# Low parts of the first products' weights: subtraction on DVE instead of POOL

## The chip, the cores and the metric

The kernel runs on one core of one Trainium2 chip. The time is device microseconds (us) from launch to end. PE is the matrix engine (TensorE), DVE the vector engine, ACT the scalar engine, POOL is GpSimd, and SP the engine that issues the DMAs. "L329" is line 329 of the kernel.

## What is computed

Attention with a memory term, then a small gated network on its output, all in fp32 (B = 4, H = 8, S = 576, D = 64):

```python
scores = q @ k.T / sqrt(D)                  # causal
a = exp(scores - rowmax); a /= a.sum(-1) + 1e-9
local = a @ v
q_p = elu(q) + 1
mem = (q_p @ M_prev) / ((q_p * z_prev).sum(-1) + 1e-6)
x = g * mem + (1 - g) * local               # g = sigmoid(beta), per head
h = (x @ w1) * (x @ w2)                     # 512 -> 1024
out = (h @ w3) @ w_out                      # 1024 -> 1024 -> 512
```

The weights are handed over as float64 words. Their 64 bits are read as pairs of 32-bit words, and the kernel itself makes fp32 numbers of them.

## The kernel before

**Pairs.** Attention runs over 16 pairs of heads (`pair_step`, four pairs for each of four batches). A pair's step writes instructions by a table, `ORDER`: transposes of the normalised scores (`t_mm`, L236, copied to SBUF by ACT in L267), the products with `v` (`pv_mm`, L283), the evacuation `fin`, and for the next pair the scores (`s_all`: L205 and L191 on PE, row maxima by L182 on DVE), the exponentials (`s_exp`, L217 on ACT), the normalisation (`s_norm`: L221, L222, L226 on DVE) and the memory term (`mem_a` to `mem_c`, `mem_t`: L138 and L139 on ACT, L144, L151 to L157 on DVE, L146 and L159 on POOL, transposes L165 on PE). `fin` evacuates a PSUM tile `x` twice: ACT writes a rounded high part (L294), DVE the rest (L295). There is one such PSUM tile, and the score tile `sx` of the next pair takes its place.

**Weights.** `w3 @ w_out` is made once (`w_gen`, L429 on PE, with high parts by L434 on ACT and low parts by L421 on DVE), beside the first batch's attention. The products with w1 and w2 (`gemm1`, L479) start with the second batch. Each operand of `gemm1` is a high part and a low part, and three products are added. Their results leave PSUM by L485 (ACT) and L488 (DVE).

**Conversion.** `conv_stages` turns a block of 128x512 float64 numbers into fp32, as a job in four stages: `load` (a DMA, L305, into `wst`), `scale` (ACT, L316, into a staging tile `wp`), `join` (DVE, L320 and L321) and `split`. Jobs 0 to 23 are w_out and w3 and have no split. Jobs 24 to 39 are w1 and w2, two for each of eight tiles `wsp`; their split writes the high part by ACT (L328) and the low part by POOL (L329). `conv_tick` moves three jobs on by one stage each, and six letters `c` in `ORDER` call it. The `wp` tiles rotate: two tiles of tag "o" (jobs 24, 25, 28, 29, 32, 33, 36 and on) and two others (26, 30, 34 and 27, 31, 35). So L316 of a job waits until L329 of the job before it in the same tile has read it. The `wst` tiles rotate by three: the load of job k waits for L321 of job k-3.

In the lists below the numbered names stand for jobs: `wp_847` is 27, `wp_989` 29, `wp_1011` 30, `wp_1026` 31, `wp_1177` 32, `wp_1185` 33, `wp_1223` 34, `wp_1231` 35, `wp_1267` 36.

**Order.** The code is written as one stream; a scheduler places each instruction in its engine's queue by priorities, and each engine then works its queue in order. `tc.high_priority` lifts L294, L295, L434, L485 and L488.

Of the kernel before, what the change touches and what calls it, by code (L numbers as in the profile page):

```python
# [13 lines left out]
ALU = mybir.AluOpType  # L14
# [23 lines left out]
def f32(ap):  # L38
    return ap.bitcast(F32)
# [3 lines left out]
def attention_moe_kernel(  # L43
# [13 lines left out]
    nc = tc.nc  # L57
# [240 lines left out]
    def conv_stages(k, src, dh, dl):  # L298
        n = 512
        box = {}  # L300

        def load():
            t = x_p.tile([128, 2 * S], F32, tag=f"x{4 + k % 3}", name="wst")
            box["raw"] = t[:, 0:2 * n].bitcast(U32).rearrange("p (n w) -> p n w", w=2)
            nc.sync.dma_start(out=t[:, 0:2 * n].bitcast(U32), in_=src.bitcast(U32))  # L305

        def scale():
            if k < 24:
                box["raw"] = raws[src[0]][:, src[1]]
            if k < 24:  # L310
                box["p"] = dh()
            elif k < 36 and k % 4 > 1:
                box["p"] = big.tile([128, n], F32, tag=f"r{4 + k % 4}", name="wp")
            else:
                box["p"] = o_p.tile([128, n], F32, tag="o", name="wp")
            nc.scalar.activation(out=box["p"], in_=f32(box["raw"][:, :, 1]), func=ACTF.Prelu, scale=2.0 ** -111, alpha=-(2.0 ** 32))  # L316

        def join():
            p = box["p"].bitcast(U32)
            nc.vector.tensor_scalar(out=p, in0=p, scalar1=3, scalar2=None, op0=ALU.logical_shift_left)  # L320
            nc.vector.scalar_tensor_tensor(  # L321
                out=p, in0=box["raw"][:, :, 0], scalar=29, in1=p, op0=ALU.logical_shift_right, op1=ALU.bitwise_or
            )

        def split():
            if k < 24:
                return
            nc.scalar.activation(out=dh(), in_=box["p"], func=ACTF.Copy)  # L328
            nc.gpsimd.tensor_tensor(out=dl(), in0=box["p"], in1=f32(dh()), op=ALU.subtract)  # L329

        return load, scale, join, split

# [216 lines left out]
    def pair_step(p, F):  # L549
# [46 lines left out]
        out=mask[:, 448:576], in_=mask[:, 448:576], pattern=[[-1, 128]], compare_op=ALU.is_ge,  # L596
# [96 lines left out]
```

## Time and profile before

| | us |
|---|---|
| median of 3 runs (lowest, highest) | 572.43 (571.6, 573.46) |
| the profiled execution | 571.37 |
| its span, first to last instruction | 569.6 |
| PE busy | 545.4 (96%) |
| DVE / ACT busy | 279.4 / 277.5 (49% each) |
| POOL busy | 126.6 (22%) |

The views below give times in us from the start of the span. A busy PE need not be a PE at its full clock; the granted clock is a column of its own, as a share of the full one.

### The profile page before, as it was taken

What the parts mean: (1) busy time and instruction counts of PE and PEld (TensorE: products, weight loads), DVE (VectorE), ACT (ScalarE), POOL (GpSimd) and SP (SyncE); (2) the same over time, 40 slices, a digit from 0 to 9 for tenths busy, and PEclk for the clock granted to TensorE, in tenths of its full rate; (3) what the DMA queues carried; (4) which work ended last, traced back from release to release, by engine and by line L of the source; (5) the groups of instructions that cost most, each with busy time, mean ns of one, the idle gap of its engine ahead of it and who ended that gap; (6) DMA issues with size and microseconds to landing.
All of it is one profiled execution on the core that took longest, in us unless ns stands there. A gap on an engine that the chain in (4) does not pass through costs nothing.

```text
span 569.6 us, 9266 instructions
## 1 busy us (share of the span) xinstructions
PE 545.4 (96%) x3440; PEld 436.4 (77%) x3440; DVE 279.4 (49%) x880; ACT 277.5 (49%) x723; POOL 126.6 (22%) x153
## 2 busy tenths in 40 slices
PE   4899897899999999999999999999999999999997
PEld 2344554456797889788988898797969797998995
DVE  6986797838662626263726272724535351111111
ACT  5565785648562546454644455444635362130210
POOL 1101333015613032303230313021310320130220
PEclk9899989799999999999999999999999999999999
DMA  7991653713021312130202121322012000001001
GB/s 292 421 379 49 223 181 121 223 48 102 31 68 29 105 29 67 34 109 29 66 20 92 29 68 34 91 64 68 26 36 99 23 1 6 33 1 38 1 1 55
DMA packets 23069, 48.31 MB, mean 85 GB/s; under 512 B 6896, under 2 KB 13040, under 8 KB 21488
## 3 DMA queue, kind: packets, MB, share of 16 engines
q1 hardware_dynamic: 23024, 47.72, 25.1%
q8 instruction: 27, 0.44, 0.3%
q14 instruction: 18, 0.15, 0.1%
HBM read 43.00 MB, written 4.72 MB: 84 GB/s over the span
## 4 chain that ended last, share of the span: by engine, by line
PE 82%; DVE 8%; ACT 4%; issue 2%; POOL 2%; DMA 2%; SPq 0%; POOLq 0%; DVEq 0%
PE m L479 36%; PE m L499 18%; PE x L283 7%; PE s L236 7%; PE s L205 4%; PE m L429 4%; PE x L274 2%; PE sx L205 2%; DVE sm L226 2%; PE x L165 1%; DVE sm L182 1%; POOL wsp L329 1%; DMA wst<-w_out 1%; ACT pt L267 1%; PE s L191 1%
## 5 line engine op out<-in xcount | busy, mean ns | idle before, releaser
L479 PE MATMUL m<-xs,wsp 128*128 128x288 f32 x1536 | 221.6, 299 | 1.3 <-DVE wL L421 1.3
L479 PEld LDWEIGHTS m<-xs,wsp 128*128 128x128 f32 x1536 | 206.7, 188 | 2.3 <-DVE wL L421 1.5
L491 POOL TENSOR_TENSOR ht<-a,ht 128x288 fp32r<-128x288 f32 (+2 forms) x96 | 57.6, 612 | 237.5 <-ACT ht L490 237.5
L217 ACT ACTIVATE sm<-sm,mx 128x320 f32<-128x320 f32 (+2 forms) x144 | 82.7, 576 | 39.5 <-DVE mx L182 38.5
L499 PE MATMUL m<-wH,ht 128*128 128x512 f32 x288 | 94.2, 396 | 0.0
L488 DVE SCALAR_TENSOR_TENSOR a<-m,a 128x288 f32<-128x288 f32 x64 | 29.1, 455 | 99.1 <-PE m L479 94.7
L267 ACT ACTIVATE pt<-s 128x512 f32<-128x512 f32 (+1 forms) x144 | 63.3, 492 | 25.1 <-PE s L236 25.0
L429 PE MATMUL m<-wo,w3s 128*128 128x512 f32 x128 | 65.5, 647 | 6.2 <-DVE w3s L321 3.8
L499 PEld LDWEIGHTS m<-wH,ht 128*128 128x128 f32 x288 | 54.1, 188 | 11.2
L490 ACT ACTIVATE ht<-a 128x288 fp32r<-128x288 f32 (+2 forms) x96 | 31.5, 360 | 63.2 <-DVE a L488 63.1
L236 PE MATMUL s<-ident,sm 128*128 128x128 f32 x448 | 61.7, 273 | 0.0
L236 PEld LDWEIGHTS s<-ident,sm 128*128 128x128 f32 x448 | 52.7, 140 | 7.2 <-issue 5.8
L226 DVE TENSOR_SCALAR sm<-sm,sums 128x320 f32<-128x320 f32 (+2 forms) x144 | 57.1, 457 | 0.4
L182 DVE CUSTOM_DVE_ANT_0 sm<-s,mask 128x320 f32<-128x320 f32 (+3 forms) x112 | 44.4, 448 | 24.4 <-PE s L205 24.3
L499 PE MATMUL m<-wL,ht 128*128 128x512 f32 x144 | 56.2, 390 | 0.0
L146 POOL TENSOR_TENSOR e<-qn,z 128x640 f32<-128x640 f32 x16 | 25.3, 1581 | 136.3 <-DVE qn L144 112.9
L485 ACT ACTIVATE a<-m 128x288 f32<-128x288 f32 x64 | 26.1, 408 | 50.7 <-PE m L479 45.4
L429 PEld LDWEIGHTS m<-wo,w3s 128*128 128x128 f32 x128 | 24.4, 209 | 31.3 <-issue 20.0
L283 PEld LDWEIGHTS x<-pt,v 128*64 128x64 f32 x384 | 25.1, 137 | 29.9 <-issue 24.0
L283 PE MATMUL x<-pt,v 128*64 128x448 f32 (+4 forms) x384 | 46.7, 393 | 0.0
L295 DVE TENSOR_TENSOR xs<-x,xs 128x576 fp32r<-128x576 f32 x16 | 12.1, 756 | 66.6 <-ACT xs L294 66.6
L205 PE MATMUL s<-raw 64*128 64x320 f32 (+3 forms) x256 | 38.3, 414 | 4.5 <-DMA raw<-qkt 4.5
(65 smaller groups left out, 474.3 us busy)
## 6 DMA issues: line engine op xcount, KB each, us to landing
raw<-qkt SPq DMA_DIRECT2D x16, 576.0 KB, 3.9
wst<-w3t SPq DMA_DIRECT2D x8, 1024.0 KB, 8.9
wst<-w SPq DMA_DIRECT2D x16, 512.0 KB, 3.8
qn<-qn SPq DMA_DIRECT2D x16, 320.0 KB, 3.0
v<-v SPq DMA_DIRECT2D x32, 160.0 KB, 2.3
out<-o SPq DMA_DIRECT2D x18, 256.0 KB, 2.0
wst<-w_out SPq DMA_DIRECT2D x4, 1024.0 KB, 12.0
z<-z_prev SPq DMA_DIRECT2D x16, 64.0 KB, 2.9
```

The source lines that it names most:

```text
L182: nc.vector.tensor_tensor_reduce(out=sm[a][c][:, lo:hi] if c else sm0[:, 0:64], in0=x, in1=mask[:, S - KE[c] + lo:S - KE[c] + hi] if c els ...
L205: nc.tensor.matmul(y, lhsT=t[r, 0, 128 * c - 64:128 * c + 64], rhs=t[r, 1, lo:hi], start=True, stop=True)
L217: nc.scalar.activation(out=x, in_=x, func=ACTF.Exp, bias=mx, scale=-1.0, accum_out=sums_of(p)[:, k:k + 1])
L226: nc.vector.tensor_scalar(out=x, in0=x, scalar1=sums_of(p)[:, k:k + 1], scalar2=None, op0=ALU.mult)
L236: tr = lambda o, c, a, kc: nc.tensor.transpose(ps[:, o:o + 128], sm[a][c][:, 128 * kc:128 * kc + 128], ident)
L267: nc.scalar.activation(out=d, in_=s, func=ACTF.Copy)
L283: nc.tensor.matmul(x[64 * a:64 * a + 64, 384 + q0:384 + q1], lhsT=vv[:, a, kc], rhs=pt[:, a, o:o + q1 - q0], start=False, stop=(q0 == 0 or ...
L429: nc.tensor.matmul(ps, lhsT=w[:, 128 * kc:128 * kc + 128], rhs=wo[:, 512 * (kc % 2):512 * (kc % 2) + 512], start=(kc == 0), stop=(kc == 7))
L479: nc.tensor.matmul(ps[:, 0:U], lhsT=w[:, i, x, j], rhs=x_t[NC * b + j][:, xx, U * u:U * u + U], start=(k == 0), stop=(k == 11))
L490: nc.scalar.activation(out=hbuf(f, 0)[:, p:p + c], in_=a[:, o:o + c], func=ACTF.Copy)
L491: nc.gpsimd.tensor_tensor(out=hbuf(f, 1)[:, p:p + c], in0=a[:, o:o + c], in1=f32(hbuf(f, 0)[:, p:p + c]), op=ALU.subtract)
L499: nc.tensor.matmul(ps, lhsT=hbuf(f, a)[:, p:p + 128], rhs=b[f], start=(k == 0), stop=(k == 23))
```

## The change

In `split` the subtraction that writes the low part (box minus high part) is issued to DVE and no longer to POOL. The operands, the tiles and the shape (128x512) are the same.

```diff
             if k < 24:
                 return
             nc.scalar.activation(out=dh(), in_=box["p"], func=ACTF.Copy)
-            nc.gpsimd.tensor_tensor(out=dl(), in0=box["p"], in1=f32(dh()), op=ALU.subtract)
+            nc.vector.tensor_tensor(out=dl(), in0=box["p"], in1=f32(dh()), op=ALU.subtract)
```

All sixteen L329 leave POOL's queue for DVE's. PE's queue keeps its order from first to last. The scheduler also moves other instructions of DVE and ACT, in three places above all.

DVE in the third pair's step, from the memory term's L152 on, up to the row maxima of the next pair's scores; `n_907` is the memory term's divisor, `xs_850` the evacuated tile. Before:

```order
L152 TENSOR_SCALAR n_907<-n_907 128x10
L153 RECIPROCAL n_907<-n_907 128x10
L157 TENSOR_TENSOR n_907<-n_907,g_sb_104 128x10
L320 TENSOR_SCALAR wp_1026<-wp_1026 128x512
L321 SCALAR_TENSOR_TENSOR wp_1026<-wst_1009,wp_1026 128x512
L320 TENSOR_SCALAR wp_1011<-wp_1011 128x512
L321 SCALAR_TENSOR_TENSOR wp_1011<-wst_987,wp_1011 128x512
L295 TENSOR_TENSOR xs_850<-x_823,xs_850 128x576
L320 TENSOR_SCALAR wp_1231<-wp_1231 128x512
L321 SCALAR_TENSOR_TENSOR wp_1231<-wst_1221,wp_1231 128x512
L320 TENSOR_SCALAR wp_1223<-wp_1223 128x512
L182 ISA sm02_109,mx_869<-s_854,mask_101 128x320
```

and with the change, with one more L329 (job 29) just ahead of the first row, and one more (job 31) between the last row and L182:

```order
L152 TENSOR_SCALAR n_907<-n_907 128x10
L329 TENSOR_TENSOR wsp_957<-wp_847,wsp_957 128x512
L153 RECIPROCAL n_907<-n_907 128x10
L320 TENSOR_SCALAR wp_1177<-wp_1177 128x512
L157 TENSOR_TENSOR n_907<-n_907,g_sb_104 128x10
L321 SCALAR_TENSOR_TENSOR wp_1177<-wst_1024,wp_1177 128x512
L320 TENSOR_SCALAR wp_1026<-wp_1026 128x512
L321 SCALAR_TENSOR_TENSOR wp_1026<-wst_1009,wp_1026 128x512
L320 TENSOR_SCALAR wp_1011<-wp_1011 128x512
L321 SCALAR_TENSOR_TENSOR wp_1011<-wst_987,wp_1011 128x512
L295 TENSOR_TENSOR xs_850<-x_823,xs_850 128x576
L329 TENSOR_TENSOR wsp_1170<-wp_1011,wsp_1170 128x512
```

The join of job 32 has moved to a place ahead of L295, and the joins of jobs 35 and 34 to places behind the first row maxima.

ACT around the evacuation L294 of the same step. Before:

```order
L328 ACTIVATE wsp_957<-wp_847 128x512
L316 ACTIVATE wp_1026<-wst_1009 128x512
L328 ACTIVATE wsp_1170<-wp_1026 128x512
L316 ACTIVATE wp_1011<-wst_987 128x512
L294 ACTIVATE xs_850<-x_823 128x576
L316 ACTIVATE wp_1231<-wst_1221 128x512
L328 ACTIVATE wsp_1170<-wp_1011 128x512
L316 ACTIVATE wp_1223<-wst_1183 128x512
```

and with the change:

```order
L316 ACTIVATE wp_1177<-wst_1024 128x512
L328 ACTIVATE wsp_957<-wp_847 128x512
L316 ACTIVATE wp_1026<-wst_1009 128x512
L316 ACTIVATE wp_1011<-wst_987 128x512
L294 ACTIVATE xs_850<-x_823 128x576
L328 ACTIVATE wsp_1170<-wp_1026 128x512
L328 ACTIVATE wsp_1170<-wp_1011 128x512
L316 ACTIVATE wp_1231<-wst_1221 128x512
```

L328 of job 31 now stands behind L294.

DVE at the end of the fourth pair's step, where L421 writes the last low part of `w3 @ w_out` (`wL7`). Before:

```order
L226 TENSOR_SCALAR sm14_115<-sm14_115,sums_1113 128x576
L421 SCALAR_TENSOR_TENSOR wL7_133<-m_1059,wH7_125 128x512
L320 TENSOR_SCALAR wp_1267<-wp_1267 128x512
L321 SCALAR_TENSOR_TENSOR wp_1267<-wst_1229,wp_1267 128x512
L320 TENSOR_SCALAR wp_1275<-wp_1275 128x512
```

and with the change:

```order
L222 RECIPROCAL sums_1113<-sums_1113 128x2
L421 SCALAR_TENSOR_TENSOR wL7_133<-m_1059,wH7_125 128x512
L226 TENSOR_SCALAR sm04_111<-sm04_111,sums_1113 128x576
L226 TENSOR_SCALAR sm14_115<-sm14_115,sums_1113 128x576
L329 TENSOR_TENSOR wsp_1260<-wp_1223,wsp_1260 128x512
L329 TENSOR_TENSOR wsp_1260<-wp_1231,wsp_1260 128x512
L320 TENSOR_SCALAR wp_1267<-wp_1267 128x512
```

L421 now stands ahead of the last two L226; two L329 (jobs 32 and 33) stand before and behind the seven L226 ahead of it.

## Rows read from the trace of the kernel before

**Rows 1.** The page, part 1: busy time of each engine.

```profile
PE 545.4 (96%) x3440; PEld 436.4 (77%) x3440; DVE 279.4 (49%) x880; ACT 277.5 (49%) x723; POOL 126.6 (22%) x153
```

**Rows 2.** Timeline of PE: start, us, engine, line, count [idle before, releaser].

```profile
71.87 1.13 PE L205 MATMUL sx<-raw 64*128 64x512 f32 x4 [2.32 <-DVE xs L295]
...
73.58 7.68 PE L429 MATMUL m<-wo,w3s 128*128 128x512 f32 x14
...
100.02 1.76 PE L205 MATMUL sx<-raw 64*128 64x512 f32 x4 [3.19 <-DVE xs L295]
...
103.73 0.69 PE L191 MATMUL s<-raw,qd 128*128 128x64 f32 x2 [1.63 <-DVE mx L182]
...
111.46 0.60 PE L236 MATMUL s<-ident,sm 128*128 128x128 f32 x4
...
127.88 5.37 PE L429 MATMUL m<-wo,w3s 128*128 128x512 f32 x12
...
137.87 1.87 PE L479 MATMUL m<-xs,wsp 128*128 128x288 f32 x12 [1.28 <-DVE wL L421]
```

**Rows 3.** Windows: busy us (instructions) by engine, then PEclk, DMA share, GB/s.

```profile
72.00:74.00 2.00, 2.00 (x11) 1.46 (x12) 2.00 (x12) 1.75 (x7) 0.78 (x1) 0.77 0.66 234
...
100.00:102.00 2.00, 1.98 (x8) 1.00 (x8) 1.93 (x2) 0.55 (x1) 1.38 (x1) 0.60 0.92 297
```

**Rows 4.** Line L329: durations min/median/max in ns, first and last start.

```profile
L329 POOL TENSOR_TENSOR wsp<-wp,wsp x16: 1263/1293/1766, 66.2 to 147.6; 128x512 fp32r<-128x512 f32 x16
```

**Rows 5.** Timeline of POOL.

```profile
88.79 1.54 POOL L146 TENSOR_TENSOR e<-qn,z 128x640 f32<-128x640 f32 x1 [6.60 <-DVE qn L144]
92.09 1.27 POOL L329 TENSOR_TENSOR wsp<-wp,wsp 128x512 fp32r<-128x512 f32 x1 [1.76 <-ACT wsp L328]
94.01 1.26 POOL L159 TENSOR_TENSOR qn<-qn,n 128x640 f32<-128x640 f32 x1 [0.66 <-DVE n L157]
...
130.99 1.38 POOL L329 TENSOR_TENSOR wsp<-wp,wsp 128x512 fp32r<-128x512 f32 x1 [8.87 <-ACT wsp L328]
```

**Rows 6.** Timeline of DVE, third pair's step.

```profile
87.89 0.83 DVE L144 SCALAR_TENSOR_TENSOR qn<-qn,e 128x640 f32<-128x640 f32 x1 [0.91 <-ACT e L139]
88.93 1.68 DVE L320 TENSOR_SCALAR wp<-wp 128x512 uint32<-128x512 uint32 x1 [0.22 <-ACT wp L316]
90.64 0.70 DVE L321 SCALAR_TENSOR_TENSOR wp<-wst,wp 128x512 uint32<-128x512 uint32 x1
...
92.11 1.28 DVE L152 TENSOR_SCALAR n<-n 128x10 f32<-128x10 f32 x1
...
99.21 0.75 DVE L295 TENSOR_TENSOR xs<-x,xs 128x576 fp32r<-128x576 f32 x1
99.88 0.42 DVE L320 TENSOR_SCALAR wp<-wp 128x512 uint32<-128x512 uint32 x1
...
110.36 2.02 DVE L226 TENSOR_SCALAR sm<-sm,sums 128x320 f32<-128x320 f32 x7
```

**Rows 7.** Timeline of DVE, second pair's step.

```profile
66.81 1.33 DVE L144 SCALAR_TENSOR_TENSOR qn<-qn,e 128x640 f32<-128x640 f32 x1 [2.88 <-ACT e L139]
...
68.51 1.91 DVE L321 SCALAR_TENSOR_TENSOR wp<-wst,wp 128x512 uint32<-128x512 uint32 x1
```

**Rows 8.** Timeline of ACT, third pair's step.

```profile
93.39 0.68 ACT L316 ACTIVATE wp<-wst 128x512 f32<-128x512 f32 x1 [1.38 <-POOL wsp L329]
```

**Rows 9.** The page, part 6: DMA issues, KB each, median us to landing.

```profile
wst<-w SPq DMA_DIRECT2D x16, 512.0 KB, 3.8
...
wst<-w_out SPq DMA_DIRECT2D x4, 1024.0 KB, 12.0
```

**Rows 10.** The page, part 5: row maxima L182; busy us, mean ns, idle before.

```profile
L182 DVE CUSTOM_DVE_ANT_0 sm<-s,mask 128x320 f32<-128x320 f32 (+3 forms) x112 | 44.4, 448 | 24.4 <-PE s L205 24.3
```

**Rows 11.** Timelines of DVE and ACT, fourth pair's step.

```profile
130.84 4.09 DVE L226 TENSOR_SCALAR sm<-sm,sums 128x320 f32<-128x320 f32 x7
...
133.42 0.58 ACT L434 ACTIVATE wH<-m 128x512 fp32r<-128x512 f32 x1
```

## The prediction

> **What bounds the kernel now.** The page first: TensorE (PE) is busy 96% of the span, DVE and ACT about half, POOL 22% [rows 1]. So a change on DVE and POOL can only matter where PE stands still. I then listed PE's instructions in order of time and looked for idle time in front of one. While the sixteen splits of this change run (66 to 149 us) PE stands four times for DVE: 2.32 us before 71.87 and 3.19 us before 100.02 (both times a score matmul into the buffer that DVE's L295 still reads), 1.63 us before 103.73 (L191, whose PSUM bank is freed by the third row maximum, L182) and 1.28 us before 137.87 (a buffer that L421 still reads) [rows 2]. Later PE is never idle for a visible time, and its order is the same in both kernels, so what is won in these four places should stay won. Two of them also cost clock: the granted clock is 0.77 in 72 to 74 us, just behind the first, and 0.60 in 100 to 102, behind the second, where full speed is 1.00 (2.4 GHz) and 0.50 is 1.2 GHz [rows 3].
>
> Then the lines of the change. L329 is sixteen POOL instructions of 1.29 us, 20.7 us in all [rows 4]. Last the timelines of DVE, POOL and ACT around the four places. They show that DVE is late there for two reasons. The reader should see them in pairs of rows. First, some DVE instructions are held as long as POOL runs: L320 takes 1.68 us (88.93) instead of 0.42 (99.88) and ends 0.28 us after POOL's L146 (88.79 + 1.54); L152, a 10-column instruction, takes 1.28 us beside the L329 that starts at 92.09 [rows 5, 6]. L144 takes 1.33 us [rows 7] against 0.83 [rows 6]. Second, L329 frees the staging tile `wp`, and ACT's next L316 waits for it, 1.38 us before 93.39; the evacuation L294, for which L295 waits, stands behind that on ACT [rows 8].
>
> **The change, part by part.** *Removed:* 20.7 us of POOL. That is nothing by itself, since no PE wait here is charged to L329. *Added:* sixteen instructions of 128x512 with two SBUF inputs on DVE. DVE has no such `tensor_tensor` in the trace; the nearest is L321 (same shape, two SBUF inputs), 0.70 us long. DVE overlaps the end of one instruction with the start of the next: behind L295, 0.75 long, the next begins 0.67 after its start [rows 6]. So I take 0.70 - 0.08 = 0.62, in all 16 x 0.62 = 9.9 us. The bounds are 0.42, that of L320, and 0.70, if nothing overlaps. The Trainium skill (VectorE: DVE Perf Modes, the section on the errata) gives 691 ns for an fp32 `tensor_tensor` of 512 columns, and in its section on the DRAIN says that the next instruction does not start before the pipe is empty. By that each L329 would cost 0.07 us more, five stand on the path below, and the result would be about 0.3 us higher, an estimate; the row, with its overlap of 0.08, decides.
>
> Whether L329 on DVE is held by POOL too, no row shows; L321 and L144 are held [rows 7], so I take it as held. If not, L295 in the first place comes another 0.5 us earlier. The Trainium skill (SBUF — State Buffer, the section on the shared port pair) says a DVE instruction with two SBUF inputs is locked out by a POOL instruction that reads SBUF, and the reverse, which would hold L329 too.
>
> *First place (before 71.87).* DVE's order becomes L329, L144, L320, L329, L151, L295. The first L329 fits into DVE's idle time before L144, so POOL does nothing beside L144, which shrinks from 1.33 to 0.83; POOL's L146 and all behind it come 0.5 us earlier. Behind L146 there now stands L329 where L321 stood, held until L146 ends, as that L321 was (1.91 us) [rows 7]; L321 goes behind L295. PE's wait falls from 2.32 to 1.8 us.
>
> *Second place (before 100.02 and 103.73).* I take the new DVE order and walk it. L144 starts at 87.4 (87.89 - 0.5), L146 0.9 later at 88.3 and ends at 89.84; L320 ends 0.28 later, 90.1. L321 and L151 take 1.47 (from 90.64 to 92.11) [rows 6]: 91.6. Then L329 0.62, L152, L329 0.62, L153, L320 0.42, L157, L321 0.63, the three small ones together 0.2: 94.1. POOL's L159 has meanwhile been let loose by L157 and takes 1.26 [rows 5]: 95.35. L320 ends 0.28 behind it, L321 0.63, L320 0.42, L321 0.63: 97.3. L295 then starts, against 99.2 before, and PE restarts at 98.0 instead of 100.02. That is in spite of one more pair L320, L321 and two L329 ahead of L295; what pays is that L152 and one L320 are no longer held, and that the loop from L321 over ACT's L328 to the freed tile is 0.7 us shorter at each L329. ACT no longer puts an L328 between its L316s and L294. Its last L316 ahead of L294 needs the load of job 30, issued when L321 is through at 90.75; at 3.8 us [rows 9] it is there at 94.55, in time.
>
> Behind L295 there are now two L329 instead of L320, a held L321 and L320, and then L182. L295 gives DVE free 0.67 after its start (99.21 to 99.88) [rows 6], at 97.95; two L329 (1.24) and three L182 at 0.45 less their overlap (1.1) [rows 10] make 100.3, where PE was let go at 103.73: about 3.5 us.
>
> Not all of it stays. PE's next need of DVE is the transpose at 111.46, which needs four of the seven L226 that start at 110.36 [rows 2, 6]; four sevenths of 2.02 is 1.15, so PE was released there with nothing to spare. Between the third L182 and L226 the new order has three L320 and two L321 against one and two, 0.9 us more; the rest is the same there, with a wait for ACT in both. So this transpose can start at 111.46 - 3.5 + 0.9 = 108.9, a gain of **2.6 us** against the old time. PE is there before: twelve L429 take 5.37 us at full clock [rows 2], so from 100.6 it is done with them at 106.0. Low clock behind the first place made fourteen of them take 7.68 instead of 14/12 x 5.37 = 6.27 us [rows 2], 1.4 us; PE can lose that once here without any effect on the sum, since it then waits that much less for DVE.
>
> *Third place (before 137.87).* L421 is the last DVE instruction of its pair step, behind seven L226 that take 4.09 instead of 2.02 us because of the L329s on POOL from 130.99 on [rows 5, 11]. Now L421 moves ahead of the last two L226: from 130.84, L329 0.62, L226 2.02, L329 0.62, small ones 0.3, L421 0.62 gives 135.0; its high part from ACT (L434, 133.42 + 0.58) is there at 134.0 [rows 11]. PE asks at 136.6. The whole **1.28 us** goes, with 1.6 to spare; next on PE are L479 products, which have their low parts by then.
>
> *Costed at nothing:* the L329s of the last jobs, between 135 and 149 us, lie beside L479 products on PE; the buffer that the L488 behind them frees is asked for only two product groups later. POOL's L146, L159 and L491 can be held by a DVE L329 for 0.6 us; PE needs L159's tile after the twelve L429 only.
>
> **Sum:** 2.6 + 1.3 = 3.9 us. The profiled execution took 571.37 us (span 569.6), which gives 567.5; the median of the runs is 1.06 above it, so I forecast 572.43 - 3.9 = **568.5 us**.
>
> **Rivals.** *The clock is kept in the first place.* With 1.8 us of standing instead of 2.32 the clock may stay at 1.00. The 1.4 us of low clock are then saved; I let 1.3 of it reach the second place, since DVE's chain there starts with work that PE paces. Time: 567.2. For: PE stands a quarter less. Against: 1.8 is near to 2.32.
>
> *Time given back on DVE.* What L152 and the other held instructions give back is filled by two L329 and one pair more, and L295 starts at 99.2 as before. Then only the third place is won: 571.1. For: POOL's L146 and L159 still hold DVE in the same stretch. Against: the walk above has them in it.
>
> *Slower: a load takes the place of POOL.* In the new DVE order the L320 of job 33 stands ahead of the row maxima for the big score tiles and so of the transposes; it needs ACT's L316, and that needs the job's load, whose buffer is freed by the L321 that ends at 97.2. At 3.8 us it lands at 101.0 and costs nothing. ACT comes to this L316 at about 101.8, behind four L217; a load that lands later moves the transpose by as much. It decides for slower than before if it lands after 105.7, 8.5 us behind its issue; at the 12.0 us of the `w_out` loads [rows 9], which shared the DMA engines with many others, the transpose comes 7.4 us later: -3.9 + 7.4 = +3.5, 575.9. For: the loads of jobs 33 to 35 and two of `v` are all issued between 94 and 98 us by this walk. Against: the median of these loads is 3.8.
>
> **How the numbers follow.** Forecast 0.60, clock kept 0.13, time given back 0.19, slower 0.08. The forecast's own spread (L329 between its bounds, held or not, one low stretch more or less behind 109) is 567 to 571. The range 566.4 to 572.0 holds all but the slower case and the ends of the others. A measurement here tells about 0.3% (1.7 us) from no change: faster is 0.13 and nearly all of the forecast, 0.70; within 0.3% is the time given back and the forecast's upper end, 0.22; slower 0.08.
>
> **What would show it.** In the changed profile: L329 on DVE at a mean of about 0.7 us, more where POOL's L146 or L159 runs; L152 never above 0.3 us beside a split; PE's waits for L295 near 1.8 and 1.7 us; L191 restarting near 100, the transpose behind it near 109 and waiting for DVE's L226; no wait for L421 behind 130 us. I am wrong if L295 of the second place still starts past 99, or if PE's new wait in front of the transpose (about 2.4 us) is charged to anything but L226.

## The result and the profile after

The changed kernel takes **567.79 us** (median of 4 runs, 566.29 to 568.69) against 572.5 us (4 runs of the kernel before beside them, 571.6 to 573.46): a ratio of **0.9915, 95% interval 0.9886 to 0.9943**, so 3.3 to 6.5 us faster. Run again later it gave 568.13 us, 0.9928 (0.9914 to 0.9942). The forecast was 568.5. The profiled execution took 568.35 us (span 566.6), 3.0 less than the profiled one of before.

The page, part 1, of the changed kernel: PE does the same work, POOL has 16 instructions fewer and DVE 16 more.

```profile
PE 545.3 (96%) x3440; PEld 435.9 (77%) x3440; DVE 280.7 (50%) x896; ACT 278.3 (49%) x723; POOL 106.0 (19%) x137
```

L329 by itself (durations in ns: smallest, median, largest; first and last start):

```profile
L329 DVE TENSOR_TENSOR wsp<-wp,wsp x16: 681/690/2035, 66.2 to 146.5; 128x512 fp32r<-128x512 f32 x16
```

Half of POOL's 1293 ns [rows 4]; DVE's busy time grows by only 1.3 us though it does 16 x 0.69 = 11 us more, because others shrink. The timeline of PE, against [rows 2]:

```profile
71.45 1.13 PE L205 MATMUL sx<-raw 64*128 64x512 f32 x4 [1.84 <-DVE xs L295]
...
73.16 7.67 PE L429 MATMUL m<-wo,w3s 128*128 128x512 f32 x14
...
98.23 1.13 PE L205 MATMUL sx<-raw 64*128 64x512 f32 x4 [1.83 <-DVE xs L295]
...
100.65 0.69 PE L191 MATMUL s<-raw,qd 128*128 128x64 f32 x2 [1.12 <-DVE mx L182]
101.13 8.18 PE L429 MATMUL m<-wo,w3s 128*128 128x512 f32 x12
...
109.69 0.60 PE L236 MATMUL s<-ident,sm 128*128 128x128 f32 x4
...
126.11 5.37 PE L429 MATMUL m<-wo,w3s 128*128 128x512 f32 x12
...
134.58 1.84 PE L479 MATMUL m<-xs,wsp 128*128 128x288 f32 x12
```

Read it as a running account against before: PE is 0.42 us ahead at the first place, 1.79 at the second L295, 3.08 at L191, and only 1.77 at the transposes (109.69 against 111.46); the lead stays 1.77 up to 126 us and is 3.29 at 134.58, where before stood 1.28 us for L421. What is lost between L191 and the transposes, 1.31 us, is clock: the twelve L429 there take 8.18 us, against 6.86 before:

```profile
104.21 6.86 PE L429 MATMUL m<-wo,w3s 128*128 128x512 f32 x12
```

Windows of the changed kernel, with the columns of [rows 3]:

```profile
72.00:74.00 2.00, 2.00 (x11) 1.30 (x8) 2.00 (x12) 2.00 (x9) 0.00 (x0) 0.66 0.00 0
100.00:102.00 2.00, 1.35 (x3) 0.92 (x4) 1.91 (x8) 2.00 (x8) 0.00 (x0) 0.50 0.91 324
106.00:108.00 2.00, 2.00 (x5) 0.86 (x4) 1.73 (x12) 1.48 (x5) 0.00 (x0) 0.81 0.98 385
108.00:110.00 2.00, 2.00 (x12) 1.23 (x11) 2.00 (x10) 0.82 (x3) 0.00 (x0) 1.00 0.10 41
```

The clock was at 0.50 (1.2 GHz) from 100.0 us to about 106.8, and the twelve L429 took 2.8 us more than the 5.37 that they take at 1.00. The kernel before had a low stretch of the same length, about 100.4 to 107.2 (0.60, 0.50, 0.50 and 0.70 in the four windows of 2 us from 100 us on), but PE stood still for 1.63 us of it; in the changed kernel PE has work all through it from 100.65 on. DVE, second and third place, against [rows 6, 11]:

```profile
87.41 0.83 DVE L144 SCALAR_TENSOR_TENSOR qn<-qn,e 128x640 f32<-128x640 f32 x1 [0.96 <-ACT e L139]
88.40 1.74 DVE L320 TENSOR_SCALAR wp<-wp 128x512 uint32<-128x512 uint32 x1 [0.16 <-ACT wp L316]
...
91.52 0.68 DVE L329 TENSOR_TENSOR wsp<-wp,wsp 128x512 fp32r<-128x512 f32 x1
92.11 0.17 DVE L152 TENSOR_SCALAR n<-n 128x10 f32<-128x10 f32 x1
92.19 0.69 DVE L329 TENSOR_TENSOR wsp<-wp,wsp 128x512 fp32r<-128x512 f32 x1
...
97.42 0.75 DVE L295 TENSOR_TENSOR xs<-x,xs 128x576 fp32r<-128x576 f32 x1
...
129.78 2.03 DVE L226 TENSOR_SCALAR sm<-sm,sums 128x320 f32<-128x320 f32 x7
...
132.47 0.68 DVE L421 SCALAR_TENSOR_TENSOR wL<-m,wH 128x512 fp32r<-128x512 f32 x1
```

L152, ten columns, is back to 0.17 us from 1.28; the seven L226 are back to 2.03 from 4.09. L320 beside L146, which stays on POOL, is held as before (1.74). On ACT, what still keeps L294 and so L295 late:

```profile
95.64 0.68 ACT L316 ACTIVATE wp<-wst 128x512 f32<-128x512 f32 x1 [2.04 <-DMA wst<-w]
96.21 0.65 ACT L294 ACTIVATE xs<-x 128x576 fp32r<-128x576 f32 x1
```

### The profile page after: what moved, and what is told of

It is laid out like the page before. It is cut to its first block, busy times and chain, and to the rows that moved or that the text cites. A ratio compares the mean times of both kernels' runs of the same rounds, so it can differ in the third digit from the quotient of the medians.

```text
span 566.6 us, 9264 instructions
## 1 busy us (share of the span) xinstructions
PE 545.3 (96%) x3440; PEld 435.9 (77%) x3440; DVE 280.7 (50%) x896; ACT 278.3 (49%) x723; POOL 106.0 (19%) x137
## 4 chain that ended last, share of the span: by engine, by line
PE 86%; DVE 6%; ACT 4%; DMA 2%; issue 1%; POOL 0%; SPq 0%; POOLq 0%; DVEq 0%; ACTq 0%
PE m L479 36%; PE m L499 18%; PE x L283 7%; PE s L236 7%; PE m L429 6%; PE s L205 5%; PE sx L205 2%; PE x L274 2%; PE x L165 2%; DMA wst<-w_out 1%; PE s L191 1%; ACT pt L267 1%; DMA wst<-w 1%; ACT sm L217 1%; DVE wo L321 1%
## 5 line engine op out<-in xcount | busy, mean ns | idle before, releaser
L479 PE MATMUL m<-xs,wsp 128*128 128x288 f32 x1536 | 221.6, 299 | 0.0
L479 PEld LDWEIGHTS m<-xs,wsp 128*128 128x128 f32 x1536 | 206.7, 188 | 0.8
L217 ACT ACTIVATE sm<-sm,mx 128x320 f32<-128x320 f32 (+2 forms) x144 | 82.6, 575 | 40.2 <-DVE mx L182 39.0
L429 PE MATMUL m<-wo,w3s 128*128 128x512 f32 x128 | 66.6, 656 | 6.6 <-DVE w3s L321 4.0
L182 DVE CUSTOM_DVE_ANT_0 sm<-s,mask 128x320 f32<-128x320 f32 (+3 forms) x112 | 44.5, 449 | 25.7 <-PE s L205 25.7
L146 POOL TENSOR_TENSOR e<-qn,z 128x640 f32<-128x640 f32 x16 | 25.3, 1582 | 156.4 <-DVE qn L144 133.0
L226 DVE TENSOR_SCALAR sm<-sm,sums 128x320 f32<-128x320 f32 (+2 forms) x144 | 54.0, 436 | 0.4
L429 PEld LDWEIGHTS m<-wo,w3s 128*128 128x128 f32 x128 | 24.7, 211 | 32.6 <-issue 20.6
L295 DVE TENSOR_TENSOR xs<-x,xs 128x576 fp32r<-128x576 f32 x16 | 12.1, 756 | 67.2 <-ACT xs L294 67.2
```

Of the source, the lines that this page charges most:

```text
L182: nc.vector.tensor_tensor_reduce(out=sm[a][c][:, lo:hi] if c else sm0[:, 0:64], in0=x, in1=mask[:, S - KE[c] + lo:S - KE[c] + hi] if c els ...
L217: nc.scalar.activation(out=x, in_=x, func=ACTF.Exp, bias=mx, scale=-1.0, accum_out=sums_of(p)[:, k:k + 1])
L226: nc.vector.tensor_scalar(out=x, in0=x, scalar1=sums_of(p)[:, k:k + 1], scalar2=None, op0=ALU.mult)
L429: nc.tensor.matmul(ps, lhsT=w[:, 128 * kc:128 * kc + 128], rhs=wo[:, 512 * (kc % 2):512 * (kc % 2) + 512], start=(kc == 0), stop=(kc == 7))
L479: nc.tensor.matmul(ps[:, 0:U], lhsT=w[:, i, x, j], rhs=x_t[NC * b + j][:, xx, U * u:U * u + U], start=(k == 0), stop=(k == 11))
```

## The experiments

My theory: the gain comes from DVE at three separate places, because POOL no longer holds DVE's instructions there and the loop over the staging tile is shorter; the clock takes part of it back. Rival A: all of it is L421's new place in DVE's order. Rival B: POOL's hold does not matter, only the order and the loop. All ratios are to the kernel before, run beside each. Where lines are added, an experiment's line numbers are up to six higher than those quoted here.

**The two halves.** One edit each on the changed kernel (the second with `k >= 32`):

```diff
-            nc.vector.tensor_tensor(out=dl(), in0=box["p"], in1=f32(dh()), op=ALU.subtract)
+            (nc.vector if k < 32 else nc.gpsimd).tensor_tensor(out=dl(), in0=box["p"], in1=f32(dh()), op=ALU.subtract)
```

> L329 on DVE for the first eight splits (66 to about 105 us), on POOL for the last eight. Theory (the gain has three places of its own, two of them in the early stretch): the two early places keep what they gave in the changed kernel's profile, 1.8 us up to the transposes at 110 us, and the wait for L421 behind 130 us, 1.28 us in the kernel before, is back: 570.0 to 571.0 us, and L295 of the second place starts near 97.4. Rival A (all that counts is L421, which moves ahead of two L226): no gain, 572 to 573. Rival B (the clock levels out whatever comes early): also 572 to 573, but with L295 at 97.4.

> L329 on POOL for the first eight splits, on DVE for the last eight. Theory: only the third place is won, 1.28 us: 571.0 to 571.6 us; PE's waits for L295 are 2.3 and 3.2 us as in the kernel before, no wait for L421 behind 130 us. Rival A (L421's place is all): the whole gain, 567.5 to 568.5. If the first part alone and the last part alone add up to the whole, the places are independent.

Early half alone: 569.51 us, 0.9954 (0.9935 to 0.9973). Late half alone: 570.77 us, 0.9974 (0.9962 to 0.9986). Both lie a little below the ranges expected (by 0.5 and 0.2 us), and L295 of the early half's second place starts at 98.12, not near 97.4. PE of the early half:

```profile
98.93 1.17 PE L205 MATMUL sx<-raw 64*128 64x512 f32 x4 [2.34 <-DVE xs L295]
...
136.43 1.87 PE L479 MATMUL m<-xs,wsp 128*128 128x288 f32 x12 [1.28 <-DVE wL L421]
```

and of the late half:

```profile
72.31 2.08 PE L205 MATMUL sx<-raw 64*128 64x512 f32 x4 [2.34 <-DVE xs L295]
...
101.70 1.13 PE L205 MATMUL sx<-raw 64*128 64x512 f32 x4 [2.93 <-DVE xs L295]
105.41 0.69 PE L191 MATMUL s<-raw,qd 128*128 128x64 f32 x2 [2.29 <-DVE mx L182]
```

Each wait follows its own half, and 0.46% and 0.26% add up to 0.72%, the gain of the changed kernel's second measurement (0.85% in the first). Within their intervals (0.2% and 0.1% either way) the places are independent, and rival A is out: almost two thirds come without L421. In the early half the seven L226 near 130 us take 4.09 us again, beside POOL's L329.

**Pieces on POOL.** The changed kernel, with POOL busy for nothing at the same places:

```diff
+    idle = const.tile([128, 96], F32, name="idle")
...
             nc.vector.tensor_tensor(out=dl(), in0=box["p"], in1=f32(dh()), op=ALU.subtract)
+            for _ in range(4):
+                hi = f32(dh())[:, 0:96]
+                nc.gpsimd.tensor_tensor(out=idle, in0=hi, in1=hi, op=ALU.subtract)
```

> The changed kernel, and at each split four small POOL subtractions (128x96, reading the high part twice, written to a scratch tile) beside L329 on DVE: POOL is busy again at the same places, but nothing waits for its result. Theory (POOL at work holds DVE): L329 and the DVE instructions next to it take longer than 0.69 us wherever POOL runs, L295 of the second place starts 1 to 2.5 us later than 97.4, and a good part of the gain is gone: 569.5 to 572.5 us. Rival B (what counts is that DVE need not hand over to POOL and back, the shorter loop of the staging tile, and L421's place, not POOL's hold): 567.5 to 568.5, with the DVE durations as in the changed kernel.

572.93 us, 1.0024 (1.0005 to 1.0043): the gain is gone, a little past the theory's end, but not in the way that I expected. PE, DVE and ACT keep their order. The profiled execution is the fastest of the twelve (570.26 us; the slowest took 577.1), so its trace does not show what the others lost beyond that. L295 of the second place starts at 96.5, not later than in the changed kernel; but here the clock stayed at 1.00 behind the first place. Its DVE timeline:

```profile
96.47 0.74 DVE L296 TENSOR_TENSOR xs<-x,xs 128x576 fp32r<-128x576 f32 x1
97.24 2.02 DVE L330 TENSOR_TENSOR wsp<-wp,wsp 128x512 fp32r<-128x512 f32 x2
...
129.00 2.55 DVE L227 TENSOR_SCALAR sm<-sm,sums 128x320 f32<-128x320 f32 x7
...
148.05 0.82 DVE L152 TENSOR_REDUCE n<-e 128x10 f32<-128x640 f32 x1 [3.46 <-POOL e L147]
```

and its POOL timeline:

```profile
91.74 5.00 POOL L333 TENSOR_TENSOR idle<-wsp 128x96 f32<-128x96 f32 x8 [2.13 <-ACT wsp L329]
...
129.80 10.68 POOL L333 TENSOR_TENSOR idle<-wsp 128x96 f32<-128x96 f32 x18
...
141.66 4.83 POOL L333 TENSOR_TENSOR idle<-wsp 128x96 f32<-128x96 f32 x8
146.45 1.56 POOL L147 TENSOR_TENSOR e<-qn,z 128x640 f32<-128x640 f32 x1
```

Beside six of the pieces, back to back, the seven L226 (here L227) take 2.55 us; beside whole L329 of 1.3 us they took 4.09 [rows 11]. One by one, two of those seven took 1.40 and 1.48 us and ended 0.19 and 0.25 us behind a whole L329, the others 0.24 to 0.44; beside the pieces none takes more than 0.53. So POOL's hold is by the instruction: pieces let DVE in between, and the largest price that this trace shows is POOL's queue. L146 (here L147) stands behind eight pieces, DVE's reduction waits 3.46 us for it, and PE waits 2.64 us behind that at 151 us. That is another mechanism than the one the run was meant to bring back; for rival B the run as a whole says only that POOL's work is not free. What speaks for the hold is the L226 rows, with the same DVE instructions, and the second place beside that of the kernel with an idle tile (below), which has the same order on PE, DVE and ACT and the same clock behind the first place. With the pieces PE is 0.54 us later at the first place and L295 0.55 us later at the second (96.47 against 95.92); the two L329 behind it, the first beside POOL's L159, then take 2.02 us instead of 1.29, and the transposes start 1.17 us later (108.84 against 107.67). How much of the change's gain is the hold and how much the new order and the shorter loop, no run separates.

**L294 first.** What is left of the second place is ACT's L294 behind an L316 that waits for a load. A data dependency moves it: ACT makes a zero from pair 2's high part, and the L316 of jobs 30 to 32 take it as bias.

```diff
+    gate = const.tile([128, 1], F32, name="gate")
...
             nc.vector.tensor_tensor(out=t[:, 1], in0=x, in1=f32(t[:, 0]), op=ALU.subtract)
+            if p == 2:
+                nc.scalar.activation(out=gate, in_=f32(t[:, 0, 0:1]), func=ACTF.Copy, scale=0.0)
...
-            nc.scalar.activation(out=box["p"], in_=f32(box["raw"][:, :, 1]), func=ACTF.Prelu, scale=2.0 ** -111, alpha=-(2.0 ** 32))
+            late = {"bias": gate} if k in (30, 31, 32) else {}
+            nc.scalar.activation(out=box["p"], in_=f32(box["raw"][:, :, 1]), func=ACTF.Prelu, scale=2.0 ** -111, alpha=-(2.0 ** 32), **late)
```

> The changed kernel, and the L316 of jobs 30, 31 and 32 take as their bias a zero that ACT makes from pair 2's high part, so that ACT takes L294 ahead of them instead of behind an L316 that waits 2.04 us for a load. Theory (what is left of the second place is L294's place on ACT and the joins ahead of L295): L295 at about 93.5 us instead of 97.4, PE's 1.83 us wait there is gone and the 1.12 us one behind it at most 0.6, the granted clock stays at 1.00 behind 98 us: 562.5 to 565.5 us. Rival (DVE has no room between 97 and 110 us, so that the transposes wait for L226 instead): L295 early, PE waiting 2 us or more in front of the transposes, 567 to 568.

565.99 us, 0.9893 (0.9874 to 0.9913), between the two. PE:

```profile
97.17 0.43 PE L192 MATMUL s<-raw,qd 128*128 128x64 f32 x2 [0.79 <-DVE mx L183]
...
105.68 0.67 PE L237 MATMUL s<-ident,sm 128*128 128x128 f32 x4 [1.99 <-DVE sm L227]
```

DVE's L295 starts at 92.36, five us earlier than in the changed kernel; the wait for it is gone and the clock is 1.00 from 70 to 110 us, but 1.99 us come back in front of the transposes. Between 94 and 104 us DVE still does the joins of some four jobs among and ahead of the row maxima and L226, and twice it stands waiting for their L316 (1.08 and 0.72 us). So the rival is right in part: DVE has too little room there.

**Joins behind L226.** Now only job 30 waits for L294; jobs 31 to 35 wait for a zero that DVE makes behind the last L226 of pair 3.

```diff
         for k in range(k0, k1):
...
+        if p == 3 and k0 == 0:
+            nc.vector.tensor_scalar(out=gate[1], in0=su[:, 0:1], scalar1=0.0, scalar2=None, op0=ALU.mult)
...
+            late = {"bias": gate[int(k > 30)]} if 30 <= k < 36 else {}
```

> The gated kernel, but only job 30 waits for L294 of pair 2; the L316 of jobs 31 to 35 take as bias a zero that DVE makes behind the last L226 of pair 3, so that no join stands between the row maxima and the L226 of that pair. Theory (in the gated kernel DVE is the bound in front of the transposes: the joins of jobs 31 to 34 take about 2.8 us there and wait for loads): no PE wait for L295 in the second place, at most 0.3 us in front of the 64-column products, none in front of the transposes (1.99 us there before), 562.0 to 564.0 us. Rival (the joins come in one lump behind 107 us and hold pair 4's step or the first products): a new PE wait of 2 us or more between 110 and 150 us, 566 to 568.

> The two gates on the kernel before, with L329 on POOL. Theory (in the second place the change pays by making DVE earlier there, and the gates do that by another way): the second place's waits are gone without the change too, and only the first place (2.3 against 1.8 us) and the third (L421, 1.28 us) are left: 1.8 us above the kernel with two gates, 564 to 566 us. Rival (POOL's splits hold DVE just as much wherever the joins go): PE waits of 2 us or more in the second place, 568 or above.

On the changed kernel: **562.2 us, 0.9826 (0.9811 to 0.9842)**, better than both kernels, as the theory said. The same gates with L329 on POOL: 565.75 us, 0.9885 (0.9866 to 0.9903). All waits of PE between 66 and 150 us with the gates and L329 on DVE:

```profile
71.47 1.13 PE L206 MATMUL sx<-raw 64*128 64x512 f32 x4 [1.82 <-DVE xs L298]
80.22 0.67 PE L239 MATMUL s<-ident,sm 128*128 128x128 f32 x4 [0.48 <-DVE sm L227]
118.37 1.13 PE L206 MATMUL sx<-raw 64*128 64x512 f32 x4 [0.60 <-DVE xs L298]
```

and with the gates and L329 on POOL:

```profile
71.92 1.13 PE L206 MATMUL sx<-raw 64*128 64x512 f32 x4 [2.33 <-DVE xs L298]
97.75 0.43 PE L192 MATMUL s<-raw,qd 128*128 128x64 f32 x2 [1.47 <-DVE mx L183]
119.30 1.13 PE L206 MATMUL sx<-raw 64*128 64x512 f32 x4 [0.34 <-DVE xs L298]
130.86 1.86 PE L485 MATMUL m<-xs,wsp 128*128 128x288 f32 x12 [1.35 <-DVE wL L427]
```

In the second place the gates bring L295 forward with either engine. The change is still worth 0.6% beside them (0.9826 against 0.9885): the first place, 1.47 us in front of the 64-column products, and L421. The time with POOL is in the range expected, but the 1.47 us stand in the second place, where none was expected.

**Two trials from there.** L146 of pair 2 on DVE (`nc.vector if p == 2 else nc.gpsimd` at that line), and jobs 34 and 35 behind L294 of pair 3 (a third gate):

> As the kernel with the two gates, and L146 of pair 2 on DVE instead of POOL, so that in the first place nothing runs on POOL and L295 comes ahead of L151. Theory: PE's first wait for L295 falls from 1.83 to 0.5 us or less and the clock stays up behind it: 1.3 us below the kernel with two gates, 560.5 to 563 us. Rival (L146 takes 0.8 us of DVE and pushes the row maxima back by as much): the wait moves to the next product and nothing is won.

> As the kernel with two gates, but jobs 34 and 35 wait for L294 of pair 3, so that their joins stand behind L295 there. Theory: the 0.60 us wait for L295 at 118.4 us goes and nothing else changes: 0.6 us below the kernel with two gates, 561.3 to 562 us. Rival (what DVE does later there it must do ahead of the third place): a new wait for L421 or in front of the first products, 562.2 us or more.

Neither helps: 562.24 us (0.9825, 0.9809 to 0.984) and 562.34 us (0.9832, 0.9818 to 0.9847). With L146 on DVE the first wait falls from 1.82 to 0.86 us, but 0.86 us for L159 at 79 us and 0.54 us for a row maximum at 96.6 are new. With the third gate the 0.60 us wait is gone and 0.74 us in front of the next pair's 64-column products stands in its place. Both went to their rivals.

**The clock.** The changed kernel once more, unedited, and with one more tile that nothing reads:

```diff
+    idle = const.tile([128, 96], F32, name="idle")
...
     nc.gpsimd.memset(md, 0.0)
+    nc.gpsimd.memset(idle, 0.0)
```

> The changed kernel once more, unedited, for its spread and its clock. In its first profile the clock fell behind both early places and cost 1.4 and 2.8 us of PE; in the profile of the gated kernel it stayed at 1.00 behind the first place after the same wait of 1.83 us. If the fall is a matter of chance at such a wait: median 567 to 569 us again, and a profile in which the waits stand (1.8, 1.8 and 1.1 us) but at least one low stretch may be missing. If the wait decides it: both low stretches again.

> The changed kernel with one more small tile that POOL clears at the start and nothing reads: the same order on PE, DVE and ACT, only addresses and one early POOL instruction differ. It is for the clock. In all five profiles without added tiles the clock fell behind the first place, in all five with one it stayed at 1.00, at waits from 1.8 to 2.7 us in both groups. If the place of the tiles or the early timing decides: no low stretch behind the first place, 566 to 568 us. If it is chance from run to run: a low stretch in about half the cases, 567.5 to 568.5 us.

The repeat showed both low stretches again in its profile. They need not be in every execution: the granted clock over the whole span was 0.985 in three of the nine executions of the changed kernel, both profiled ones among them (568.35 to 568.42 us), and 0.990 to 0.993 in the other six (566.29 to 568.69). The kernel with a tile (566.28 us, 0.9907, 0.9888 to 0.9926) has the same order on PE, DVE and ACT, but its clock stayed at 1.00 behind the first place. Its PE:

```profile
71.73 1.13 PE L206 MATMUL sx<-raw 64*128 64x512 f32 x4 [1.83 <-DVE xs L296]
...
96.73 1.13 PE L206 MATMUL sx<-raw 64*128 64x512 f32 x4 [0.99 <-DVE xs L296]
99.15 0.43 PE L192 MATMUL s<-raw,qd 128*128 128x64 f32 x2 [1.12 <-DVE mx L183]
...
107.67 0.67 PE L237 MATMUL s<-ident,sm 128*128 128x128 f32 x4 [0.64 <-DVE sm L227]
```

and its DVE:

```profile
95.92 0.75 DVE L296 TENSOR_TENSOR xs<-x,xs 128x576 fp32r<-128x576 f32 x1
96.70 1.29 DVE L330 TENSOR_TENSOR wsp<-wp,wsp 128x512 fp32r<-128x512 f32 x2
```

The same 1.83 us wait, no low clock behind it; PE is 1.5 us earlier than in the changed kernel's profile at the second place, and 2.0 earlier at the transposes, with a wait for L226. What an added tile has to do with it stays open: the next run has one too, and its clock fell. One profile of it cannot tell the tile from chance; and of the five profiles with a tile that the expectation counts, the one with L146 on DVE had a wait of 0.86 us only, not 1.8.

**L421 behind L226.** The changed kernel, with the last L421 taking its factor from a value made behind the two last L226:

```diff
+        if p == 4 and k0 == 0:
+            x = sm[1][4][:, KE[4] - 1:KE[4]]
+            with tc.high_priority(200):
+                nc.vector.tensor_scalar(out=unit, in0=x, scalar1=0.0, scalar2=2.0 ** -16, op0=ALU.mult, op1=ALU.add)
...
+            with tc.high_priority(200 if i == NF - 1 else 0):
...
-                out=wL[i], in0=box.pop(i), scalar=2.0 ** -16, in1=f32(wH[i]), op0=ALU.mult, op1=ALU.subtract
+                    out=wL[i], in0=box.pop(i), scalar=unit if i == NF - 1 else 2.0 ** -16, in1=f32(wH[i]), op0=ALU.mult, op1=ALU.subtract
```

> The changed kernel, but the last L421 takes its factor 2^-16 from a value that DVE makes behind the two last L226 of that pair, so that it stands behind both of them, one L321 and one L329, with POOL idle. Theory (the third place is won because L421 moved ahead AND the L226 are no longer held; DVE's work ahead of L421 sets it): L421 ends near 135.7 us where PE asks at 134.6, a wait of about 1.1 us for L421 is back, 569 to 569.5 us. Rival (only POOL's hold on the L226 counted): no wait, 567.8 to 568.3 us.

566.77 us, 0.9903 (0.9885 to 0.9921), and no wait for L421. It doesn't answer the question: L421 ends at 134.90, but PE's second group of L479 begins at 133.87, before that, right behind the ACT instruction that reads the first group (133.42 + 0.40). So PE did not stand for what L421 reads here, presumably because the group got the other bank. Whether L421's order alone would have done stays open. In its profiled execution (567.61 us, 0.7 below the changed kernel's) the clock behind the second place fell for less long than in the changed kernel, and PE then waited for L226:

```profile
101.09 6.72 PE L435 MATMUL m<-wo,w3s 128*128 128x512 f32 x12
...
108.86 0.67 PE L241 MATMUL s<-ident,sm 128*128 128x128 f32 x4 [0.50 <-DVE sm L227]
```

At this place PE is 0.83 us ahead of the changed kernel (109.69).

## Why the prediction was right, step by step

- **The cost of L329 on DVE** (0.62 a piece, bounds 0.42 and 0.70). The next instruction starts 0.59 to 0.61 us behind it (91.52 to 92.11; two in 1.22 us at 98.20). The row's overlap decided: DVE's next instruction starts before the 0.69 us are over. The Trainium skill (VectorE: DVE Perf Modes, the section on the DRAIN) has the pipe empty first, but adds that a next instruction that is not held starts earlier; the prediction used the first statement alone, and the trace agrees with the second.
- **L329 held by POOL.** Taken as held, and it is: the one beside L146 (67.96; POOL 67.79 to 69.45) takes 2.04 us. Here the trace agrees with the Trainium skill (SBUF — State Buffer, the shared port pair); so do the pieces above, where the hold ends with each POOL instruction.
- **First place**: wait of 1.8 us predicted, 1.84 measured.
- **Second place**: L295 at 97.3 predicted, 97.42 measured; PE at 98.0, measured 98.23; L191 at 100.2 to 100.3, measured 100.65. Inside that walk one step was off: job 30's load was to land "in time" at 94.55. It landed at about 95.6, 4.6 us behind its issue, and ACT stood 2.04 us for it. It cost little because DVE's queue ahead of L295 was full to 96.1 anyway, as the walk had it.
- **The transposes** were the mis-sized term: 108.9 and a gain of 2.6 us predicted, with PE waiting 2.4 us for L226 and one low stretch of 1.4 us hidden in that wait. Measured in the profile: 109.69, a gain of 1.77, and no wait, so the sign that the prediction named, about 2.4 us charged to L226, was not there. The clock stayed at 0.50 for 6.8 us and made PE's work 2.8 us longer, twice what the prediction had allowed for. It delayed DVE as well, which the prediction did not have:

```profile
106.60 0.60 ACT L434 ACTIVATE wH<-m 128x512 fp32r<-128x512 f32 x1 [0.52 <-PE m L429]
107.23 0.69 DVE L421 SCALAR_TENSOR_TENSOR wL<-m,wH 128x512 fp32r<-128x512 f32 x1 [0.27 <-ACT wH L434]
108.30 2.02 DVE L226 TENSOR_SCALAR sm<-sm,sums 128x320 f32<-128x320 f32 x7
```

  L226 is behind an L421 whose high part waits for an L429 at the low clock. In the L421 experiment the low stretch cost PE 1.35 us (6.72 against 5.37), these two waits are not there, L226 starts at 107.90, and the step came out as written: 108.86 with a wait for L226. So of the 2.8 us 0.83 reached the time (109.69 against 108.86), since PE came that much later than DVE let it; the rest was hidden, as the prediction had it for one stretch.
- **Third place**: the 1.28 us are gone, as predicted; the late half alone is worth 0.26%, 1.5 us.
- **The sum**, 3.9 us: 3.0 in the two profiled executions, 3.3 to 6.5 by the interval of the first measurement, 4.1 by the repeat's ratio. That the profiles show less than the medians is mostly that the profiled execution of before lay 1.1 us below its median. The third place and most of the walk were right in size; the second place's 2.6 would be 1.8 by the profile. By the profiles the sum was 0.9 us too high, so that the forecast came within 0.7 us of both medians is in part luck.
- **The rivals.** *Clock kept in the first place*: it did not happen in either profile of the changed kernel, but it did in the one with an idle tile, and the step that I gave it, 1.3 us reaching the second place, was about right: 1.5 us there. *Time given back on DVE* fell with L295 at 97.42. *A load takes POOL's place*: the later L316s waited for DVE's L329 (1.41 us at 99.58) or followed ACT's L217, none of them 8 us for a load.

## What to carry to other kernels

Short work that moves from POOL to DVE can let DVE come earlier to the instruction that counts, though it has more to do, where POOL's whole instructions hold DVE's neighbours: look for tiny DVE instructions that take as long as a POOL instruction. Then ask which transfer or conversion stands in an engine's queue ahead of the one instruction that another engine waits for; a false data dependency (a zero bias) moved it, and was worth somewhat more than the change here (0.9928 to 0.9826), but only once the rest of that work was out of the chain too. Where PE still stalls, the clock behind the stall is a term of its own: here up to 2.8 us of PE's work, of which 0.8 us showed in the time where PE would else have waited. It belongs into the range rather than into the sum.

## What was not expected of the hardware

- POOL's hold on DVE is by the instruction: seven L226 take 2.03 us alone, 2.55 us beside six short POOL instructions back to back, 4.09 us beside whole L329s.
- The length of PE's wait at the first place does not decide whether the clock falls: it fell behind waits of 1.83 and 1.84 us (changed kernel, its repeat, the L421 experiment) and stayed at 1.00 behind 1.82 and 1.83 us (gated kernels, idle tile), behind 2.33 us (gates with POOL) and 2.67 us (pieces). What does is open.
- A stretch of low clock can outlast the wait by far: 6.8 us at 0.50 from the second of the waits of 1.83 and 1.12 us on. It made PE's work 2.8 us longer, but only some 0.8 us of that reached the time.
